# Placing transposed probabilities from two DMA queues in an attention and SoLU layer kernel

## The chip, the cores and the metric

The kernel runs on one core of one Trainium2 chip. The metric is the time of one execution on the device in microseconds (us), as the median of several runs. Beside the runs there is one execution recorded by the hardware profiler; its span, from the first to the last instruction, is what the views of the profile divide.

The core has five engines that each work through their own list of instructions in order: TensorE (PE, the matmuls), VectorE (DVE), ScalarE (ACT), GpSimd (POOL) and SyncE (SP, which only starts DMAs here). They meet through semaphores. ScalarE can start DMAs too.

## What is computed

Block-causal attention over 8 batches, 8 heads, 576 positions and 64 dimensions per head, and on its output, as 4608 tokens of 512, a layer with SoLU and a normalization:

```python
def _attn_ref(q, k, v):                       # (8, 8, 576, 64) each
    scores = scale * np.matmul(q, k.transpose(0, 1, 3, 2))
    mask = block_i >= block_j                 # blocks of 64 positions
    scores = np.where(mask, scores, -1000000000.0)
    scores = scores - np.max(scores, axis=-1, keepdims=True)
    attn = np.exp(scores)
    attn = attn / (np.sum(attn, axis=-1, keepdims=True) + 1e-09)
    return np.matmul(attn, v)

def _moe_ref(x, w_in, w_out, g_ln):           # x is (4608, 512), d_ff is 1024
    h = x @ w_in
    e = np.exp(h - np.max(h, axis=-1, keepdims=True))
    solu = h * e / (np.sum(e, axis=-1, keepdims=True) + 1e-09)
    ln = (solu - mean) / np.sqrt(var + 1e-06) * g_ln
    return ln @ w_out
```

The weights and g_ln come as float64 words and are taken apart on the chip.

## The kernel before, in words

**Two kinds of work.** Attention runs by pairs of heads, the layer by tiles of 128 tokens. A pair is two heads of one batch, so there are 32 pairs and 36 tiles. The four pairs of the first batch are worked in two parts (part 0 and part 1) so that the layer can begin early; the 28 pairs behind them are whole. This text numbers the pairs 0 to 31.

**A pair** (function `attention`): q and k are loaded and split into a high and a low part (`kh`, `kl`, `qh`, `ql`); PE forms the scores in groups of one query block of 128 rows per head (lines 567 and 573, written in this text as S128, S256, S384, S512 by their width, and L for the 64 last rows of both heads). DVE takes each row's maximum (L602), ACT the exponential with the row sum (L614), DVE adds and inverts the sums (L624, L625), and the probabilities `pb` are scaled by POOL, ACT or DVE (L632, L634, L633). For the AV product they are needed transposed. The first 8 entries (the parts of batch 0) are transposed by PE (L554). For the other 28 pairs DVE transposes 32x32 blocks in place (two instructions, L640: 12 and 13 slots of 128 columns), and four DMAs of 400 KB place the quarters of `pb` into the tile `pt` (L648, in `place`). PE then multiplies (L660, function `avmm`, 52 matmuls a pair in two results `av0` and `av1`), and ACT copies the results into the tile `xt` (L412, `copy`): one copy of 128x384 for `av0`, and three for `av1` (64x192, 64x128 and 64x64), because `av1`'s two halves stood at different columns. `pt`, `pb` and `vr` (the values v) have two buffers each, used in turn.

**A tile** (function `moe`): `xt` is split into `xh` and `xl` (L721, L725); two times 12 matmuls with w_in (L746, "H" here); maximum, exponential, product, mean (L752 to L761); the square sum on ACT (L764); DVE transposes 32x32 blocks (L782), four DMAs place them into `ct` (L786); `ct` is split into `ch` and `cl` (L794, L798); two times 12 matmuls with w_out (L816, "O" here); the result leaves through `ob` (L820, L822).

**What sets the order.** All operations are handed to `Schedule.op` with an engine (and others that could do it, `alts`), a duration, what they read and write, and a key. `Schedule.run` is a planner: it walks through a model of the five engines in time, and whenever an engine is free it gives it the ready operation with the smallest key. The keys are the number of the pair or tile plus a value of the table PARAMS. The order so found is the order in which the instructions are written, for every engine; nothing is chosen on the chip. For a DMA the planner holds a duration of the issue, a duration on the DMA engines (`dma`) and a latency (`tail`). Four placements were planned as 4 x 600 ns of issue, 6800 ns of transfer and 3200 ns of latency.

**Queues.** Before the change every DMA but the very first stands on SP's queue: loads of q, k (four DMAs each, 144 KB) and v, placements of `pt` (4 a pair) and of `ct` (4 a tile), and the results. What stands ahead in this queue must have been issued before the next one is.

The functions that the change touches, and what calls them:

Of the kernel before, what the change touches and what calls it, by code (L numbers as in the profile page):

```python
# [14 lines left out]
I32 = mybir.dt.int32  # L15
# [16 lines left out]
NPT = 2  # L32
# [5 lines left out]
DEPTH = 2500.0  # L38
SLACK = 120.0
START = {"PE": 0.0, "ACT": 2930.0, "DVE": 0.0, "POOL": 2500.0, "SP": 560.0}  # L40
PARAMS = {
# [6 lines left out]
    "a_sp": 15.151, "a_sp32": 33.434, "a_lf": -19.843, "a_w": -53.076, "a_xh": 7.699, "a_xl": 42.171,  # L48
    "a_c": 45.045, "a_o": 1.147, "np": 32, "l0": 10.919, "a_cl": 82.304, "a_ai": -19.611, "aff": -198.558,
    "a_t3": -226.025, "a_cm": -13.873, "a_cg": -136.828, "a_sa": -14.146, "a_sa32": 226.312, "a_qh": -1.948,  # L50
    "a_kl": -33.0, "a_ch": 8.609, "a_chd": 185.089, "a_clo": -87.939, "ct0": -0.422, "qA": -20.741,
    "qeA": -57.386, "sA": -4.436, "seA": -5.607, "srA": 89.822, "spA": 243.774, "ptA": 46.328, "peA": -58.037,
    "avA": 18.17, "aeA": 50.13, "ldA": -276.676, "lvA": 10.694, "a_spA": -0.83, "a_saA": 1.199, "w2": 5.397,
    "w3": 49.83, "hA": 84.857,
}
# [6 lines left out]
class Schedule:  # L62
# [49 lines left out]
    def run(self):  # L112
# [20 lines left out]
        while events:  # L133
# [18 lines left out]
            for e in engs:  # L152
# [46 lines left out]
                if best.dma > 0.0:  # L199
                    dmafree = max(t + min(best.dur, 600.0), dmafree) + best.dma  # L200
                    engfree[e] = max(done, dmafree - DEPTH)
                    done = max(engfree[e], dmafree)
                heapq.heappush(events, (done + best.tail, n, 1, best, None))
# [8 lines left out]
def kernel(  # L212
# [53 lines left out]
    wid[LAST] = S  # L266
    soff = {(0, 0): 0, (0, 1): 1, (0, 2): 3, (1, 0): 6, (1, 1): 7, (1, 2): 9, (0, 3): 12, LAST: 16, (1, 3): 21}
    NSL, NSA = 25, 12
# [57 lines left out]
    def t_act(n, extra=0.0):  # L326
        return n / 1.2 + 51.0 + extra
# [16 lines left out]
    def rows(dst, src):  # L344
        for r_ in range(4):
            SP.dma_start(dst[r_::4], src[r_])
# [7 lines left out]
    def prep(i, src, hi, lo, gcol, name, key):  # L354
# [7 lines left out]
        op("ACT", 520, lambda: ACT.activation(T3.bitcast(I32), raw[:, :, 0], AF.Copy, scale=2.0**-29), r=[kr_], w=[k3], key=key,  # L362
           alts=[("POOL", 640, lambda: POOL.tensor_scalar(out=T3.bitcast(I32), in0=raw[:, :, 0], scalar1=2.0**-29, scalar2=1.0, op0=ALU.mult, op1=ALU.mult), K["a_t3"])])
# [18 lines left out]

    op("SP", 4 * 500, lambda: rows(gt, g_ln.rearrange("(c r j) -> r j c", r=4, j=32)), w=["gt"], key=K["w2"], tail=2100)
    n = 0
# [25 lines left out]
    def copy(which, n_, aps, scale, w, key, ps, r=()):  # L410

        op("ACT", t_act(n_), lambda: ACT.activation(aps()[0], aps()[1], AF.Copy, scale=scale), r=r, w=w, key=key, ps=ps,  # L412
           alts=[("DVE", t_dve(n_), lambda: DVE.tensor_scalar(out=aps()[0], in0=aps()[1], scalar1=scale, scalar2=None, op0=ALU.mult), K[f"e{which}"])])
# [29 lines left out]
    def attention(p, pair, part=None):  # L443
# [86 lines left out]
        for x, z, hi, lo, scale in () if peq or part == 0 else (("k", kz[:, zs], kh_, kl_, 1.0), ("q", qz[:, zs], qh_, ql_, 0.125)):  # L530
            zk = (x + "z", zs)
            op("DVE", t_dve(S) + 30, lambda z=z: DVE.transpose(z, z), r=[zk], w=[zk], key=kk)
            op("ACT", t_act(S), lambda z=z, hi=hi, scale=scale: ACT.activation(hi, z, AF.Copy, scale=scale), r=[zk], w=[(x + "h", iq)], key=ke,
               alts=[("POOL", 0.836 * S + 243, lambda z=z, hi=hi, scale=scale: POOL.tensor_scalar(out=hi, in0=z, scalar1=scale, scalar2=1.0, op0=ALU.mult, op1=ALU.mult), K["a_qh"])])
# [24 lines left out]
        for g, (kind, us, masks) in enumerate(groups):  # L559
# [57 lines left out]
            if g in zlast:  # L617
# [9 lines left out]
                zk = [("z", i, u) for u in bs]  # L627
                op("DVE", 300, recip, r=zk, w=[("rz", i, zg)] + zk, key=p + K["sr" + sfx])
                for b in bs:
# [14 lines left out]
        if not pep:  # L644

            def place():
                for a_ in (0, 2, 1, 3):
                    SP.dma_start(pt_[:, a_].rearrange("p s i -> p (s i)"), pb[32 * a_ : 32 * a_ + 32].rearrange("p r s i -> p (r s i)"))  # L648

            op("SP", 4 * 600, place, r=tk, w=ptk, key=p + K["pe" + sfx], tail=3200, dma=6800)  # L650

# [5 lines left out]
        def avmm():  # L657
# [28 lines left out]
            for j in range(5):  # L686
                for h in range(2):
                    if j < 4:
                        sl = slice(12 + j, 17 + j, 4) if h == 0 else slice(16 + j, 22 + j, 5)
                        mm(av1, h, low(0), j, 2 * h, 2 * h + 2, sl, j == 0, False)  # L690
                    else:
                        mm(av1, h, flat(128 - 128 * h, 2), j, 2 * h, 2 * h + 2, 20, False, True)
            for j in range(4):
                for h in range(2):
                    mm(av1, h, flat(64, 2), j, 2 - 2 * h, 4 - 2 * h, 12 + 9 * h + j, j == 0, j == 3)

        d = 660 if part == 0 else 2500 if part else 2835
# [177 lines left out]
```

## Time and profile before

| | |
|---|---|
| runs, us | 731.9, 723.35, 724.76 |
| median, us | 724.76 |
| profiled execution, us | 728.37 |
| its span, us | 726.6 |
| mean granted TensorE clock | 0.974 |
| bytes read from and written to HBM | 37.23 MB, 9.44 MB |
| DMA packets on SP's queue, their share of 16 engines | 222320, 74.9% |
| matmuls, weight loads | 4747, 4747 |

The profiled execution took 728.37 us, 1.8 us more than its span; it is 0.5% above the median of the three runs and lies between them. Times in the views are counted in us from the span's start. A row that groups instructions gives the line, the engine, the operation and its tiles, the count, the busy time in us with the mean of one in ns, and behind the last bar the idle time of the engine just before them with what ended it. A row of the timeline gives start, duration, and in square brackets the idle time ahead of it.

### The profile page before, as it was taken

To read this page: it belongs to the slowest core of one execution; us is meant where nothing else is said; L and a number is where in the kernel's file an instruction comes from. 1 tells how busy PE (TensorE), PEld (TensorE's weight loads), DVE (VectorE), ACT (ScalarE), POOL (GpSimd) and SP (SyncE) were. 2 spreads that over 40 slices of the span, in tenths; PEclk is the share of its full clock that TensorE was granted. 3 is DMA by queue.
4 is the path that set the end of the run, shared out by engine and by line. 5 is a ranking of instruction groups with operands and counts; after the bars stand their busy time and mean duration, and the time that the engine had idled before them with its cause. 6 is when DMAs were issued, how large, how long until landed. Compare 5 with 4: busy or idle time off the path is not lost.

```text
span 726.6 us, 14364 instructions
## 1 busy us (share of the span) xinstructions
PE 673.5 (93%) x4747; PEld 530.2 (73%) x4747; DVE 574.3 (79%) x1252; ACT 499.8 (69%) x1286; POOL 359.6 (49%) x512
## 2 busy tenths in 40 slices
PE   5687897999999999989999999999989999999997
PEld 4565575777777777767777777777767777788885
DVE  2798989896999888978798979698878977455552
ACT  3686889686878867767786778587857885444432
POOL 1367566443665454546555554556456555223211
PEclk8598989999999999999999999999999999999999
DMA  9855358596969897969896989797969767322221
GB/s 172 195 96 130 99 114 141 123 130 169 165 170 174 213 176 194 155 166 172 203 172 163 176 205 158 173 187 180 179 160 188 171 167 168 105 72 72 73 73 44
DMA packets 223434, 109.74 MB, mean 151 GB/s; under 512 B 186496, under 2 KB 202368, under 8 KB 223360
## 3 DMA queue, kind: packets, MB, share of 16 engines
q1 hardware_dynamic: 222320, 108.56, 74.9%
q8 instruction: 37, 0.61, 0.4%
q10 hardware_dynamic: 1040, 0.26, 0.2%
q14 instruction: 37, 0.30, 0.1%
HBM read 37.23 MB, written 9.44 MB: 64 GB/s over the span
## 4 chain that ended last, share of the span: by engine, by line
PE 55%; DVE 12%; DMA 12%; ACT 9%; SPq 6%; issue 3%; POOL 2%; DVEq 0%; ACTq 0%; POOLq 0%
PE ps L816 20%; PE ps L746 16%; PE ps L660 9%; PE ps L573 6%; DMA pt<-pb 5%; ACT pb L614 3%; PE ps L567 3%; DVE nm L602 2%; DMA kz<-in_k_dram 2%; SPq L648 2%; DVE pb L640 2%; ACT pb L634 2%; DMA ct<-zb 2%; SPq L461 2%; DMA ub<-in_moe_w_in_dram 1%
## 5 line engine op out<-in xcount | busy, mean ns | idle before, releaser
L614 ACT ACTIVATE pb<-ps,nm 128x384 f32<-128x384 f32 (+4 forms) x288 | 157.1, 555 | 74.2 <-DVE nm L602 58.6
L602 DVE TENSOR_REDUCE nm<-ps 128x1 f32<-128x384 f32 (+4 forms) x288 | 132.1, 505 | 0.4
L640 DVE STREAM_TRANSPOSE pb<-pb 128x1536 f32<-128x1536 f32 (+1 forms) x56 | 101.6, 1829 | 11.4 <-ACT pb L634 7.8
L660 PE MATMUL ps<-pt,vr 128*64 128x128 f32 (+1 forms) x1648 | 92.6, 269 | 12.9 <-DMA ct<-zb 7.1
L660 PEld LDWEIGHTS ps<-pt,vr 128*64 128x64 f32 x1648 | 81.8, 137 | 30.8 <-issue 12.7
L634 ACT ACTIVATE pb<-pb,rz 128x512 f32<-128x512 f32 (+4 forms) x185 | 92.1, 566 | 17.4 <-DVE rz L625 14.5
L746 PE MATMUL ps<-wih,xh 128*128 128x512 f32 x288 | 84.3, 414 | 3.7 <-ACT pb L614 3.7
L798 POOL TENSOR_TENSOR cl<-ct,ch 128x512 fp32r<-128x512 f32 x40 | 51.6, 1293 | 71.0 <-ACT ch L794 69.0
L632 POOL TENSOR_SCALAR pb<-pb,rz 128x512 f32<-128x512 f32 (+4 forms) x101 | 63.9, 644 | 40.3 <-DVE rz L625 17.1
L816 PE MATMUL ps<-woh,ch 128*128 128x512 f32 x288 | 80.7, 402 | 0.0
L746 PE MATMUL ps<-wil,xh 128*128 128x512 f32 x288 | 79.5, 398 | 0.0
L816 PE MATMUL ps<-woh,cl 128*128 128x512 f32 x288 | 78.8, 395 | 0.0
L746 PE MATMUL ps<-wih,xl 128*128 128x512 f32 x288 | 78.7, 395 | 0.0
L816 PE MATMUL ps<-wol,ch 128*128 128x512 f32 x288 | 78.7, 395 | 0.0
L761 POOL TENSOR_SCALAR ub<-ub,ms 128x1024 f32<-128x1024 f32 x31 | 35.7, 1151 | 82.7 <-DVE ms L755 68.5
L573 PE MATMUL ps<-kh,qh 64*128 64x128 f32 (+3 forms) x256 | 58.3, 386 | 11.4 <-ACT pb L614 7.5
L746 PEld LDWEIGHTS ps<-wih,xh 128*128 128x128 f32 x288 | 50.9, 190 | 23.8 <-issue 8.6
L746 PEld LDWEIGHTS ps<-wil,xh 128*128 128x128 f32 x288 | 54.8, 190 | 13.0
L746 PEld LDWEIGHTS ps<-wih,xl 128*128 128x128 f32 x288 | 54.3, 189 | 13.1 <-POOL xl L725 0.3
L816 PEld LDWEIGHTS ps<-woh,cl 128*128 128x128 f32 x288 | 54.2, 188 | 12.8
L816 PEld LDWEIGHTS ps<-wol,ch 128*128 128x128 f32 x288 | 54.2, 188 | 12.8
L816 PEld LDWEIGHTS ps<-woh,ch 128*128 128x128 f32 x288 | 51.5, 188 | 11.4 <-ACT pb L614 0.4
(124 smaller groups left out, 1299.3 us busy)
## 6 DMA issues: line engine op xcount, KB each, us to landing
pt<-pb SPq DMA_DIRECT2D x112, 400.0 KB, 6.1
ct<-zb SPq DMA_DIRECT2D x124, 128.0 KB, 2.7
out_dram<-ob SPq DMA_DIRECT2D x36, 256.0 KB, 3.1
vr<-in_v_dram SPq DMA_DIRECT2D x64, 128.0 KB, 3.8
qz<-in_q_dram SPq DMA_DIRECT2D x56, 144.0 KB, 4.7
kz<-in_k_dram SPq DMA_DIRECT2D x56, 144.0 KB, 3.9
ub<-in_moe_w_in_dram SPq DMA_DIRECT2D x8, 512.0 KB, 6.6
ub<-in_moe_w_out_dram SPq DMA_DIRECT2D x16, 256.0 KB, 3.2
```

The source lines that it names most:

```text
L567: PE.matmul(t[:, 192 + k0 : 192 + k1], w_, x_[:, k0:k1], start=n_ == 0, stop=n_ == 2)
L573: PE.matmul(PS(sps[h])[:, off : off + 128 * (i_ + 1)], w_[half[h], 128 * i_ : 128 * i_ + 128], x_[half[h], 0 : 128 * (i_ + 1)], start=n_ = ...
L602: op("DVE", t_dve(wid[u]), lambda sp=sp, off=off, u=u: DVE.tensor_reduce(out=nm_[u], in_=PS(sp)[:, off : off + wid[u]], axis=AX.X, op=ALU. ...
L614: ACT.activation(dst, src, AF.Exp, bias=nm_[u], accum_out=z_[zg][:, zc : zc + 1])
L632: op("POOL", 0.836 * nn + 243, lambda b=b, zg=zg, zc=zc: POOL.tensor_scalar(out=puv(pb, b, pep), in0=puv(pb, b, pep), scalar1=rz_[zg][:, z ...
L634: ("ACT", t_act(nn, 133), lambda b=b, zg=zg, zc=zc: ACT.activation(puv(pb, b, pep), puv(pb, b, pep), AF.Copy, scale=rz_[zg][:, zc : zc + 1 ...
L640: op("DVE", 1.058 * 128 * (s1 - s0) + 86, lambda s0=s0, s1=s1: DVE.transpose(pb[:, :, s0:s1, :], pb[:, :, s0:s1, :]), r=[("P", i, b) for b ...
L660: PE.matmul(dst(PS(av)[half[h]]), w_, pt_[:, a0:a1, sl, :], start=start, stop=stop)
L746: PE.matmul(o_, a_[:, c, :], w_[:, c, s_], start=(si == 0 and c == 0), stop=(si == 2 and c == NKI - 1))
L761: op("POOL", 1097, lambda: POOL.tensor_scalar(out=dst, in0=src, scalar1=m[:, 3:4], scalar2=1.0, op0=ALU.add, op1=ALU.mult), r=[uk, ("m3", ...
L798: alts=[("POOL", 1225, lambda c_=c_, h_=h_, l_=l_: POOL.tensor_tensor(out=l_, in0=c_, in1=h_.bitcast(F32), op=ALU.subtract), K["a_clo"])])
L816: PE.matmul(o_, a_[:, c, :], w_[:, c, :], start=(hf == 0 and si == 0 and c == 0), stop=(hf == 1 and si == 2 and c == 7))
```

## The change

Three things are changed.

1. **Placement.** `place` becomes two operations: SP issues the DMAs of quarters 0 and 1, ACT those of quarters 2 and 3. Both read what the four read. The AV product waits for both.
2. **One copy for `av1`.** The slots of `pb` and the columns of `av1` are numbered anew, so that both halves of `av1` hold 192 columns in the same order, and one copy of 128x192 takes the place of three. The number of matmuls is the same.
3. **Planner.** Some durations are corrected, the DMA engines' time of a pair of placements is now 2400 ns, the latency 2600 ns, an issue on ACT does not hold ACT for the transfer; the whole table PARAMS has other values, so the order changes on every engine.

The core of the diff:

```diff
-    soff = {(0, 0): 0, (0, 1): 1, (0, 2): 3, (1, 0): 6, (1, 1): 7, (1, 2): 9, (0, 3): 12, LAST: 16, (1, 3): 21}
+    soff = {(0, 0): 0, (0, 1): 1, (0, 2): 3, (1, 0): 6, (1, 1): 7, (1, 2): 9, (0, 3): 12, (1, 3): 16, LAST: 20}
...
                     dmafree = max(t + min(best.dur, 600.0), dmafree) + best.dma
-                    engfree[e] = max(done, dmafree - DEPTH)
-                    done = max(engfree[e], dmafree)
+                    if e == "SP":
+                        engfree[e] = max(done, dmafree - DEPTH)
+                    done = max(done, dmafree)
...
-            def place():
-                for a_ in (0, 2, 1, 3):
-                    SP.dma_start(pt_[:, a_].rearrange("p s i -> p (s i)"), pb[32 * a_ : 32 * a_ + 32].rearrange("p r s i -> p (r s i)"))
-
-            op("SP", 4 * 600, place, r=tk, w=ptk, key=p + K["pe" + sfx], tail=3200, dma=6800)
+            def place(eng, a0):
+                for a_ in (a0, a0 + 1):
+                    eng.dma_start(pt_[:, a_].rearrange("p s i -> p (s i)"), pb[32 * a_ : 32 * a_ + 32].rearrange("p r s i -> p (r s i)"))
+
+            op("SP", 1200, lambda: place(SP, 0), r=tk, w=ptk, key=p + K["pe" + sfx], tail=2600, dma=2400)
+            op("ACT", 1050, lambda: place(ACT, 2), r=tk, w=[("ptB", p % NPT)], key=p + K["pf" + sfx], tail=2600, dma=2400)
...
-        for av, rows, parts in ((av0, both, [first]), (av1, half[0], [(0, 384, 192)]), (av1, half[1], [(64, 384, 128), (0, 512, 64)])):
-            for c_, q_, l_ in parts if av else ():
+        for av, rows, (c_, q_, l_) in ((av0, both, first), (av1, both, (0, 384, 192))):
+            if av:
```

The order of the instructions, at three places. Numbers behind a tile's name tell its buffers apart (`pb_88` and `pb_89`, `pt_90` and `pt_91`); line numbers of the changed kernel are 1 higher up to L649 and 4 higher from L725 on.

**SP's queue, two pairs in the steady middle.** `out_dram` is a tile's result, `ct<-zb` the placement in the layer. Before:

```order
L648 DMA pt_91<-pb_89 128x1x800 x4
L822 DMA out_dram<-ob_131 128x512
L786 DMA ct<-zb 128x1x256 x4
L461 DMA kz<-in_k_dram 32x36x32 x4
L461 DMA qz<-in_q_dram 32x36x32 x4
L472 DMA vr_81<-in_v_dram 128x4x64 x2
L476 DMA vr_81<-in_v_dram 64x2x64
L648 DMA pt_90<-pb_88 128x1x800 x4
```

The changed kernel, at the same place:

```order
L649 DMA pt_91<-pb_89 128x1x800 x2
L826 DMA out_dram<-ob_131 128x512
L790 DMA ct<-zb 128x1x256 x4
L462 DMA kz<-in_k_dram 32x36x32 x4
L462 DMA qz<-in_q_dram 32x36x32 x4
L473 DMA vr_81<-in_v_dram 128x4x64 x2
L477 DMA vr_81<-in_v_dram 64x2x64
L649 DMA pt_90<-pb_88 128x1x800 x2
```

The order on SP is the same; two placements of each pair have left it.

**ACT, the steady middle, around the copies of one AV product.** `ub` is the exponential of a layer tile, `nm_24` belongs to the group L, the other `nm` to the groups S. Before:

```order
L412 ACTIVATE xt_118<-ps_63 128x384
L412 ACTIVATE xt_118<-ps_64 64x192
L412 ACTIVATE xt_118<-ps_64 64x128
L412 ACTIVATE xt_118<-ps_64 64x64
L614 ACTIVATE pb_88,z_1_111<-ps_61,nm_24_100 128x5x4x32
L820 ACTIVATE ob_131<-ps_65,ms_133 128x512
```

The changed kernel, at the same place of a pair:

```order
L413 ACTIVATE xt_120<-ps_64 128x384
L413 ACTIVATE xt_120<-ps_65 128x192
L649 DMA pt_90<-pb_88 128x1x800 x2
L757 ACTIVATE ub,ms_132<-ps_61,ms_132 128x1024
L615 ACTIVATE pb_89,z_1_113<-ps_62,nm_24_109 128x5x4x32
L615 ACTIVATE pb_89,z_0_112<-ps_66,nm_02_103 128x3x4x32
```

ACT now issues two placements right behind the copies of the AV product of the pair before; the exponentials of the next pair and of a layer tile stand behind them.

**ACT, the start of the kernel.** `ob<-ub` takes apart the first weights as soon as they have arrived. Before:

```order
L614 ACTIVATE pb_88,z_0_110<-ps_63,nm_00_92 128x128
L362 ACTIVATE ob_131<-ub 128x512
L614 ACTIVATE pb_88,z_0_110<-ps_64,nm_11_97 128x256
L366 ACTIVATE zb<-zb 128x512
L412 ACTIVATE kh_84<-ps_66 128x256
L412 ACTIVATE qh_82<-ps_66 128x256
L614 ACTIVATE pb_88,z_0_110<-ps_64,nm_10_96 128x128
```

The changed kernel, from the same exponential on:

```order
L615 ACTIVATE pb_88,z_0_110<-ps_63,nm_00_92 128x128
L615 ACTIVATE pb_88,z_0_110<-ps_64,nm_11_97 128x256
L615 ACTIVATE pb_88,z_0_110<-ps_64,nm_10_96 128x128
L635 ACTIVATE pb_88<-pb_88,rz_0_114 128x256
L413 ACTIVATE kh_84<-ps_66 128x256
L413 ACTIVATE qh_82<-ps_66 128x256
L413 ACTIVATE pt_90<-ps_64 128x4x96
```

The work on the weights no longer stands between the exponentials of the first pair; on ACT it comes 13 instructions later. On SP the first load of w_in, which stood ahead of g_ln and the first loads of v, now stands behind them.

Who does what changes as well. Counted over the whole order: scalings of `pb` go from 101 on POOL, 185 on ACT and 2 on DVE to 27, 159 and 102; `ch<-ct` from 62 on ACT to 21 on ACT, 32 on POOL and 9 on DVE; the 36 copies `ob<-ps` of the layer's result from 27 on ACT and 9 on DVE to 36 on ACT.

More of the change, by code (lines that the diff above doesn't have):

```diff
@@ L41 @@
 PARAMS = {
[6 rows of a table removed]
[L48 to L54, printed above, removed]
[6 rows of a table added]
+    "e2": 6.854, "a_sp": -5.24, "a_sp32": -2.39, "a_lf": 392.26, "a_w": -42.859, "a_xh": -1.838,
+    "a_xl": -1.31, "a_c": 108.552, "a_o": 24.452, "np": 32, "l0": -2.145, "a_cl": 58.245, "a_ai": -18.732,
+    "aff": 163.937, "a_t3": -246.666, "a_cm": 104.43, "a_cg": -6.932, "a_sa": -81.936, "a_sa32": -235.294,
+    "a_qh": -173.369, "a_kl": 2.08, "a_ch": -31.735, "a_chd": -13.936, "a_clo": -282.32, "ct0": 158.564,
+    "qA": 77.049, "qeA": 0.58, "sA": -293.262, "seA": -14.134, "srA": -1.22, "spA": -15.414, "ptA": 6.678,
+    "peA": 111.138, "avA": 29.198, "aeA": 156.22, "ldA": -86.586, "lvA": -114.061, "a_spA": -9.618,
+    "a_saA": -115.183, "w2": -69.111, "w3": -46.994, "hA": 532.627, "pf": 8.694, "pf32": -9.701, "pfA": 16.29,
 }
@@ L361, in prep @@
         high = raw[:, :, 1].bitcast(F32)
-        op("ACT", 520, lambda: ACT.activation(T3.bitcast(I32), raw[:, :, 0], AF.Copy, scale=2.0**-29), r=[kr_], w=[k3], key=key,
+        op("ACT", 570, lambda: ACT.activation(T3.bitcast(I32), raw[:, :, 0], AF.Copy, scale=2.0**-29), r=[kr_], w=[k3], key=key,
            alts=[("POOL", 640, lambda: POOL.tensor_scalar(out=T3.bitcast(I32), in0=raw[:, :, 0], scalar1=2.0**-29, scalar2=1.0, op0=ALU.mult, op1=ALU.mult), K["a_t3"])])
@@ L381, in prep @@
         wkeys.append((name, "l"))
-    op("SP", 4 * 500, lambda: rows(gt, g_ln.rearrange("(c r j) -> r j c", r=4, j=32)), w=["gt"], key=K["w2"], tail=2100)
+    op("SP", 4 * 500, lambda: rows(gt, g_ln.rearrange("(c r j) -> r j c", r=4, j=32)), w=["gt"], key=K["w2"], tail=2100, dma=2800)
     n = 0
@@ L410, in copy @@
     def copy(which, n_, aps, scale, w, key, ps, r=()):
-        op("ACT", t_act(n_), lambda: ACT.activation(aps()[0], aps()[1], AF.Copy, scale=scale), r=r, w=w, key=key, ps=ps,
+        op("ACT", t_act(n_, 100 if n_ < 200 else 0), lambda: ACT.activation(aps()[0], aps()[1], AF.Copy, scale=scale), r=r, w=w, key=key, ps=ps,
            alts=[("DVE", t_dve(n_), lambda: DVE.tensor_scalar(out=aps()[0], in0=aps()[1], scalar1=scale, scalar2=None, op0=ALU.mult), K[f"e{which}"])])
@@ L532, in attention @@
             op("DVE", t_dve(S) + 30, lambda z=z: DVE.transpose(z, z), r=[zk], w=[zk], key=kk)
-            op("ACT", t_act(S), lambda z=z, hi=hi, scale=scale: ACT.activation(hi, z, AF.Copy, scale=scale), r=[zk], w=[(x + "h", iq)], key=ke,
+            op("ACT", t_act(S, 44), lambda z=z, hi=hi, scale=scale: ACT.activation(hi, z, AF.Copy, scale=scale), r=[zk], w=[(x + "h", iq)], key=ke,
                alts=[("POOL", 0.836 * S + 243, lambda z=z, hi=hi, scale=scale: POOL.tensor_scalar(out=hi, in0=z, scalar1=scale, scalar2=1.0, op0=ALU.mult, op1=ALU.mult), K["a_qh"])])
@@ L627, in attention @@
                 zk = [("z", i, u) for u in bs]
-                op("DVE", 300, recip, r=zk, w=[("rz", i, zg)] + zk, key=p + K["sr" + sfx])
+                op("DVE", 300, recip, r=zk, w=[("rz", i, zg)] + zk, key=p + K["sr" + sfx], port=True)
                 for b in bs:
@@ L666, in low, with flat2 @@
                 return lambda t: t[:, c0 : c0 + 256].rearrange("p (s a i) -> p a s i", s=2, a=4)[:, 0:2]
+            def flat2(c0):
+                return lambda t: t[:, c0 : c0 + 128].rearrange("p (s a i) -> p a s i", s=2, a=2)
             def flat(c0, n_):
@@ L688, in avmm @@
                     if j < 4:
-                        sl = slice(12 + j, 17 + j, 4) if h == 0 else slice(16 + j, 22 + j, 5)
-                        mm(av1, h, low(0), j, 2 * h, 2 * h + 2, sl, j == 0, False)
+                        mm(av1, h, low(0) if h == 0 else flat2(64), j, 2 * h, 2 * h + 2, slice(12 + 4 * h + j, 21 + j, 8 - 4 * h), j == 0, False)
                     else:
-                        mm(av1, h, flat(128 - 128 * h, 2), j, 2 * h, 2 * h + 2, 20, False, True)
+                        mm(av1, h, flat(128, 2), j, 2 * h, 2 * h + 2, 24, False, True)
             for j in range(4):
                 for h in range(2):
-                    mm(av1, h, flat(64, 2), j, 2 - 2 * h, 4 - 2 * h, 12 + 9 * h + j, j == 0, j == 3)
+                    mm(av1, h, flat(64 - 64 * h, 2), j, 2 - 2 * h, 4 - 2 * h, 12 + 4 * h + j, j == 0, j == 3)
         d = 660 if part == 0 else 2500 if part else 2835
-        op("PE", d, avmm, r=ptk + [("pt2", p % NPT, s_) for s_ in slots] + ([("v0", c) for c in range(2)] + [("qz", c) for c in range(2)] if part == 0 else [f"vr{i}"]), key=kk, opens=av0 if part == 0 else (av0, av1), mode=1)
+        op("PE", d, avmm, r=ptk + [("pt2", p % NPT, s_) for s_ in slots] + [("ptB", p % NPT)] + ([("v0", c) for c in range(2)] + [("qz", c) for c in range(2)] if part == 0 else [f"vr{i}"]), key=kk, opens=av0 if part == 0 else (av0, av1), mode=1)
         both = slice(0, P)
         first = {None: (0, 0, 384), 0: (0, 0, 256), 1: (256, 256, 128)}[part]
-        for av, rows, parts in ((av0, both, [first]), (av1, half[0], [(0, 384, 192)]), (av1, half[1], [(64, 384, 128), (0, 512, 64)])):
-            for c_, q_, l_ in parts if av else ():
+        for av, rows, (c_, q_, l_) in ((av0, both, first), (av1, both, (0, 384, 192))):
+            if av:
                 w_ = [("xt", b0 % XB, hp, rows.start, q0) for q0 in (0, 256, 384, 512) if q_ <= q0 < q_ + l_]
@@ L715, in moe @@
         m = ms[i]
-        pieces = [(0, 0, 256), (0, 256, 384), (0, 384, 576), (64, 384, 512), (64, 512, 576)]
+        pieces = [(0, 0, 256), (0, 256, 384), (0, 384, 576)]
         xk = [("xt", x, hp, r0, q0) for x, a0, a1, _, _ in segs for hp in range(NP) for r0, q0, q1 in pieces if q0 < a1 and q1 > a0]
```

12 rows, old and new, of the table PARAMS are left out of this document.

## The prediction

> **What bounds the kernel now.** I read the page's first part, then the windows by stage, then PE's waits in the longest stage.
>
> ```profile
> span 726.6 us, 14364 instructions
> PE 673.5 (93%) x4747; PEld 530.2 (73%) x4747; DVE 574.3 (79%) x1252; ACT 499.8 (69%) x1286; POOL 359.6 (49%) x512
> ```
>
> ```profile
> 0.00:40.00 40.00, 25.73 (x237) 21.96 (x239) 22.42 (x66) 20.00 (x63) 11.27 (x25) 0.70 0.81 167
> 40.00:140.00 100.00, 83.17 (x685) 64.43 (x686) 92.63 (x210) 80.53 (x205) 63.61 (x82) 0.93 0.58 121
> 140.00:200.00 60.00, 58.68 (x424) 45.72 (x423) 49.00 (x113) 45.65 (x125) 28.56 (x47) 1.00 0.87 152
> 200.00:600.00 400.00, 383.84 (x2801) 300.17 (x2800) 342.22 (x746) 300.56 (x798) 221.32 (x314) 1.00 0.92 177
> 600.00:727.00 127.00, 122.11 (x607) 97.93 (x606) 68.08 (x122) 53.05 (x100) 34.81 (x47) 1.00 0.32 87
> ```
>
> The columns are the stretch, its length, the busy time of PE, PEld, DVE, ACT and POOL, the granted clock, the DMA engines' share and GB/s. PE bounds the kernel: 93% of the span. Its idle time is 53.1 us (726.6 - 673.5), and the change leaves the matmuls as they are, so that is all there is to gain. It lies at the start (14.3 us up to 40 us, 16.8 up to 140), in the steady stage from 200 to 600 (16.2) and at the end (4.9). From 40 to 140 DVE is busier than PE (92.63 against 83.17).
>
> In the steady stage PE's own waits are these:
>
> ```profile
> PE ps L660 <- DMA ct<-zb: 7.1, 4, 2.6
> PE ps L660 <- DMA pt<-pb: 4.1, 4, 1.2
> PE ps L573 <- ACT pb L614: 3.5, 7, 1.5
> PE ps L567 <- DVE ub L754: 1.2, 1, 1.2
> ```
>
> 11.2 of the 16.2 us are the AV product's (L660), eight times, 2.6 us at most. AV does not read `ct`; the first row is the same wait put down to a DMA that landed a little later. One such wait, followed back through SP's queue:
>
> ```profile
> 404.30 3.57 DVE L640 STREAM_TRANSPOSE pb<-pb 128x1536 f32<-128x1536 f32 x2 [0.26 <-ACT pb L634]
> ...
> 425.28 2.92 PE L660 MATMUL ps<-pt,vr 128*64 128x128 f32 x50 [1.17 <-DMA pt<-pb]
> ```
>
> ```profile
> 398.79 1.79 SPq L822 DMA_DIRECT2D out_dram<-ob  x1
> 400.69 3.63 SPq L786 DMA_DIRECT2D ct<-zb  x4
> 404.41 2.78 SPq L461 DMA_DIRECT2D kz<-in_k_dram  x4
> 407.30 4.16 SPq L461 DMA_DIRECT2D qz<-in_q_dram  x4
> 411.56 1.62 SPq L472 DMA_DIRECT2D vr<-in_v_dram  x2
> 413.23 0.64 SPq L476 DMA_DIRECT2D vr<-in_v_dram  x1
> 413.97 5.70 SPq L648 DMA_DIRECT2D pt<-pb  x4
> ```
>
> DVE has both transposes done at 407.87, but SP starts the placement at 413.97, 6.1 us late: it was issuing what stands ahead, and just before this stretch stand the four placements of the pair before. AV then starts at 425.28, 1.17 us late. So AV waits for SP's queue. One placement by itself:
>
> ```profile
> 413.97 0.56 SPq L648 DMA_DIRECT2D pt<-pb  x1
> ```
> ```profile
> 414.57 0.63 SPq L648 DMA_DIRECT2D pt<-pb  x1
> ```
> ```profile
> 415.26 3.16 SPq L648 DMA_DIRECT2D pt<-pb  x1
> ```
> ```profile
> 418.46 1.20 SPq L648 DMA_DIRECT2D pt<-pb  x1
> ```
>
> The first two issues take 0.56 and 0.63 us, the third is held 3.16 and the fourth 1.20: behind two placements the queue takes no more until the first has moved.
>
> **The change part by part.**
>
> *SP.* The third and fourth issue leave SP: 3.16 + 1.20 = 4.36 us a pair. The order on SP is otherwise the same, so the placement after this stretch can begin 4.36 us sooner, at 409.6 and not 413.97, still behind the transposes (407.87). The longest AV wait is 2.6 us, so all eight go if the rest stays. I take 10 of the 11.2 us. Bounds: 0 if landing, not issue, sets the wait; 11.2 if all go.
>
> *ACT's issues.* 56 DMAs. The nearest rows are the first two issues above and ACT's only one:
>
> ```profile
> 0.72 0.47 ACTq L435 DMA_DIRECT2D xt<-in_k_dram  x1
> ```
>
> At 0.59 each (mean of 0.56 and 0.63) they are 33 us of ACT; 26 at the low row. If ACT met the held issues, a pair would cost 4.36 and not 1.19 us (the first rows' sum), 89 us more over 28 pairs; I take the low price, since the third issue is held behind two on its own queue, and ACT's queue gets only two a pair. The issue waits for DVE's transposes. Behind it on ACT stand the exponential of a layer tile and those of the next pair's L and S384, for whose PSUM PE waits. Their maxima stand behind the transposes on DVE as well, so this wait adds little: 0, with the issue time of 1.2 us a pair hidden under the AV-to-scores work of PE.
>
> *ACT's other work.*
>
> ```profile
> L412 ACT ACTIVATE xt<-ps 64x192 f32<-64x192 f32 x32 | 10.2, 318 | 2.5 <-PE ps L660 2.4
> L412 ACT ACTIVATE xt<-ps 64x128 f32<-64x128 f32 x32 | 8.7, 272 | 0.4
> L412 ACT ACTIVATE xt<-ps 64x64 f32<-64x64 f32 x32 | 6.6, 208 | 0.0
> L794 ACT ACTIVATE ch<-ct 128x512 fp32r<-128x512 f32 x62 | 38.8, 629 | 8.5 <-DMA ct<-zb 6.0 <-PE ps L816 2.2 <-issue 0.3
> ```
>
> Three copies (25.5 us in all) become one of the first row's width: 32 x 0.318 = 10.2, so 15 us are saved. 41 `ch` leave ACT: 41 x 0.629 = 26 us. The issues add 33. ACT ends within some 15 us of now and was busy 300.56 of 400 us in the steady stage: nothing on the path, as PE's work covers it; with no cover, the copy of `av1` alone would free its PSUM bank 0.48 us sooner a pair.
>
> *DVE.* 100 more scalings of `pb`. The rows that price them:
>
> ```profile
> L633 DVE TENSOR_SCALAR pb<-pb,rz 128x256 f32<-128x256 f32 x1 | 0.3, 346 | 0.0
> L633 DVE TENSOR_SCALAR pb<-pb,rz 128x128 f32<-128x128 f32 x1 | 0.3, 286 | 0.0
> L369 DVE TENSOR_SCALAR ct<-ct 128x512 uint32<-128x512 uint32 x8 | 3.4, 423 | 0.0
> L821 DVE TENSOR_SCALAR ob<-ps,ms 128x512 f32<-128x512 f32 x9 | 6.5, 721 | 0.0
> ```
>
> At 0.36 (the widths lie between the first and third row) 36 us, less 9 x 0.721 = 6.5 for the `ob` copies that leave, plus 9 `ch` at 0.42: about 33 us, some 28 of it in the steady stage: 342.22 becomes 370 of 400, 93%. In sum it fits under PE's 384; what it may cost is a maximum that comes late. I take 2 us, bounds 0 and 28 (1 us in each pair). POOL loses 74 scalings and stays under its 221 of 400: 0.
>
> *The start.*
>
> ```profile
> 22.85 0.47 PE L554 MATMUL ps<-ident,pb 128*128 128x128 f32 x1 [9.29 <-ACT pb L634]
> ```
> ```profile
> 16.22 0.68 ACT L362 ACTIVATE ob<-ub 128x512 int32<-128x512 uint32 x1 [3.62 <-DMA ub<-in_moe_w_in_dram]
> ```
> ```profile
> 5.73 1.53 SPq L350 DMA_DIRECT2D ub<-in_moe_w_in_dram  x2
> 7.30 2.77 SPq L346 DMA_DIRECT2D gt<-in_moe_g_ln_dram  x4
> ```
>
> PE's longest wait, 9.29 us, ends with a scaling that stood behind ACT's work on the weights; ACT itself sat 3.62 us for their DMA, between two exponentials of the first pair. In the new order that work comes after the first scalings, so the first transposes can start earlier. Against it, the weights are loaded behind g_ln (2.77 us of issue) and v, and up to 140 us DVE has little to spare. Bounds: 9.3 gained (the whole wait) and 2.8 lost (all that follows the weights later by g_ln's issue). I take 4 gained, a little under the middle between the whole gain and none.
>
> *The AV matmuls* keep number and size: 0. The other waits of the steady stage, 4.7 us, I leave as they are.
>
> *Sum* against the profiled execution: 728.4 - 10 + 2 - 4 = 716.4. That execution was 3.6 us above the median of the runs (724.76), so the forecast for the median is **713 us**: 12 us less. A change of 2%, 14.5 us, is about what a measurement of this kernel can tell from none; that is below 710.3 or above 739.3.
>
> **The rivals.**
>
> *The start gains more.* The first 9.29 us wait goes wholly, and with it lost clock:
>
> ```profile
> 14.00:37.50 23.50, 13.12 (x94) 10.95 (x96) 16.78 (x47) 13.62 (x45) 7.49 (x8) 0.50 0.81 168
> ```
>
> The clock is halved from the wait on: 13.12 us of PE work at 0.50 could have been 6.6. For it: the wait's cause is moved away. Against it: DVE. Start 14 in place of 4: 703 us. (The Trainium skill, "TensorE: Matmul & The Clock Gate", Part 1, says that an idle window of about 3.4 us halves the clock; this trace agrees with the half clock behind a 9.29 us wait. By that rule a wait of some 2 us would leave the clock whole.)
>
> *The transfers are no faster, the wait stays.* Over one placement and the loads around it the DMA engines are full:
>
> ```profile
> 414.00:425.20 11.20, 10.12 (x47) 7.39 (x47) 10.46 (x22) 9.55 (x25) 7.28 (x9) 1.00 0.95 206
> ```
>
> At a share of 0.95 two queues move nothing sooner, and what SP issues next is held instead. Half or more of AV's wait stays and only the start gains: 713 + 9 = 722 us. Against it: the late start on SP, which is not a transfer. The Trainium skill, "DMA: Bandwidth & Descriptors", section "Issuing engines are not separate DMA queues", states this rule: DMAs from several engines run on the same 16 engines, and several issuers save only the issue time. The trace's 0.95 agrees. By that rule only the 4.36 us of issue are saved, which in my sum is already all that counts.
>
> *Slower: DVE's transposes as one block.* In the new order both transposes of a pair stand together (3.57 us as above) behind the five scalings that ACT and DVE share, and ahead of the maxima of the next tile and pair. If that block ends late, the exponentials, the PSUM banks and then PE's next scores and H matmuls are late in each of 28 pairs. It decides from 0.43 us a pair (then the 12 us are gone) and makes the kernel slower by over 2% from 0.95. At 1 us a pair: 713 + 28 = 741 us. For it: DVE at 93%. Against it: now there is only one wait of 1.2 us of that kind (L567).
>
> *Slower still: ACT meets the held issue.* 89 us more on ACT, of which its 99 idle us in the steady stage cover about half: 713 + 44 = 757 us. Against it: the first two issues of each pair on SP are short though other DMAs run.
>
> **How the numbers follow.** Forecast 713, from 706 to 720: 0.42. Start gains more, 703: 0.20. Wait stays, 722: 0.18. DVE's block, 741: 0.12. Held issue, 757: 0.05. Something else near no change: 0.03. Faster by over 2%: 0.20 and 0.4 of the forecast's 0.42 (the part of its 14 us band below 710.3, rounded up), 0.37. Slower: 0.05 and three quarters of 0.12, 0.14. Same: the rest, 0.49. The range goes from 699 (the start's rival less 4) to 732 (the wait's rival and ten more, which takes in some of DVE's block): it leaves out 0.05, most of 0.12 and a few hundredths below.
>
> **What would show it.** Right: AV's waits for DMAs in the steady stage under 3 us in all; SP's two issues about 0.6 each and ACT's two as well; `pt` issued within 3 us of the transposes' end in every pair; PE's wait before the first L554 (now L555) under 4 us. Wrong: ACT issues of 1.2 to 3 us; PE's waits for ACT's exponentials or DVE's maxima over 15 us in the steady stage; DVE busy less than 350 of 400 us there with the time still longer; a start as long as now, with DVE waiting for w_in.

## The result, and the profile after

| | before | changed |
|---|---|---|
| median of the runs (us) | 725.56 | 798.02 |
| lowest and highest (us) | 723.35 to 731.9 | 791.06 to 801.71 |
| profiled execution: time, span (us) | 728.4, 726.6 | 801.71, 799.6 |
| PE busy, idle (us) | 673.5, 53.1 | 696.4, 103.2 |
| mean granted clock | 0.974 | 0.942 |

The changed kernel takes 1.0971 times as long (95% interval 1.088 to 1.1062): 9.7% slower, where 1.7% faster was forecast and the range ended at 732. The head of the changed kernel's page, and its windows (columns as in the prediction):

```profile
span 799.6 us, 14182 instructions
PE 696.4 (87%) x4747; PEld 547.1 (68%) x4747; DVE 579.3 (72%) x1343; ACT 467.6 (58%) x1178; POOL 326.9 (41%) x465
```
```profile
0.00:40.00 40.00, 29.34 (x287) 23.78 (x287) 23.17 (x75) 25.99 (x78) 10.31 (x25) 0.83 0.77 166
40.00:140.00 100.00, 83.06 (x651) 65.73 (x652) 89.88 (x207) 80.87 (x195) 46.65 (x64) 0.90 0.53 111
140.00:200.00 60.00, 53.35 (x387) 41.27 (x386) 46.37 (x110) 39.64 (x110) 16.79 (x26) 0.94 0.81 149
200.00:600.00 400.00, 351.07 (x2441) 273.81 (x2440) 309.78 (x719) 237.70 (x614) 190.52 (x267) 0.96 0.83 158
600.00:800.00 200.00, 179.60 (x987) 142.50 (x985) 110.11 (x235) 83.37 (x182) 62.61 (x85) 0.96 0.45 99
```

PE has as many matmuls as before (x4747), but 50 us more idle time, most of it in the steady stage: 48.9 of 400 us idle (400 - 351.07), before 16.2. Another 15 us came up behind 600 us: 20.0 us idle (199.6 - 179.60), before 4.9. The rest of the 73 us of span is a lower clock: 673.5 x 0.974 and 696.4 x 0.942 are both 656.0, so the 23 us more of busy time are the same work at a lower clock.

PE's waits in the steady stage (us in total, times, longest):

```profile
PE ps L662 <- DMA pt<-pb: 19.7, 9, 4.9
PE ps L820 <- ACT pb L615: 15.3, 7, 3.2
PE ps L750 <- ACT pb L615: 6.6, 3, 2.9
PE ps L574 <- ACT pb L615: 4.3, 1, 4.3
```

AV's waits for the placement (L662), which were to go, grew from 11.2 to 19.7 us, and the waits for ScalarE's exponentials (L615) grew from 3.5 to 26 us. Two rows on SyncE's queue and one on ScalarE tell where both begin:

```profile
SPq L473 <- DMA pt<-pb: 48.5, 10, 5.6
SPq L477 <- DMA pt<-pb: 12.4, 9, 1.8
```
```profile
ACT ob L768 <- DMA out_dram<-ob: 91.2, 28, 7.7
```

The first two rows did not exist before: SyncE's loads of v (L473, L477) wait for placements. They do not read `pt`. In the traces every DMA of this program reports its landing on one of eight semaphores, which go round over the DMAs of both queues, and waits until the one that had its semaphore last has landed. ScalarE's two placements now take two of the eight. The third row was 26.8 us before (14 times): the square (L768) writes to the scratch `ob`, whose result a store is still reading. One placement shows the first of the two; here are the transposes on DVE, ScalarE's issues, and SyncE's queue:

```profile
401.29 3.56 DVE L641 STREAM_TRANSPOSE pb<-pb 128x1536 f32<-128x1536 f32 x2
```
```profile
404.88 1.21 ACTq L649 DMA_DIRECT2D pt<-pb  x2
```
```profile
404.31 5.93 SPq L473 DMA_DIRECT2D vr<-in_v_dram  x2
411.97 0.65 SPq L477 DMA_DIRECT2D vr<-in_v_dram  x1
412.71 1.20 SPq L649 DMA_DIRECT2D pt<-pb  x2
414.01 2.68 SPq L826 DMA_DIRECT2D out_dram<-ob  x1
416.78 4.21 SPq L790 DMA_DIRECT2D ct<-zb  x4
```

ScalarE issues its half as soon as the transposes end (404.85). SyncE's second load of v has the semaphore of ScalarE's first placement, its third load that of the second, so both stand until these have landed, and SyncE's own half goes out at 412.71, 7.8 us after the other: the halves go one after the other. In 15 of the 28 pairs SyncE's half begins 4 us or more behind ScalarE's. In all, SyncE stood 72.8 us in 23 such waits. Where no such load stands ahead, both queues issue together, and ScalarE is held:

```profile
426.92 3.00 ACTq L649 DMA_DIRECT2D pt<-pb  x2
```

The first issue took 0.59, the second 2.38 us. Over 28 pairs the issues took ScalarE 49.4 us, in 10 pairs for more than 2 us.

### The profile page after: what moved, and what is told of

It reads as the page before. It is cut to its first block, busy times and chain, and to the rows that moved or that the text cites. A ratio compares the mean times of both kernels' runs of the same rounds, so it can differ in the third digit from the quotient of the medians.

```text
span 799.6 us, 14182 instructions
## 1 busy us (share of the span) xinstructions
PE 696.4 (87%) x4747; PEld 547.1 (68%) x4747; DVE 579.3 (72%) x1343; ACT 467.6 (58%) x1178; POOL 326.9 (41%) x465
## 4 chain that ended last, share of the span: by engine, by line
PE 30%; DMA 28%; DVE 14%; ACT 12%; SPq 7%; issue 5%; ACTq 2%; POOL 2%; DVEq 0%; POOLq 0%
PE ps L820 12%; DMA pt<-pb 10%; DMA out_dram<-ob 10%; PE ps L662 7%; PE ps L750 6%; ACT pb L615 5%; DMA qz<-in_q_dram 3%; DVE nm L603 3%; DVE pb L641 3%; PE ps L574 3%; SPq L462 2%; ACTq L649 2%; ACT pb L635 2%; ACT ob L768 2%; DVE kz L533 1%
## 5 line engine op out<-in xcount | busy, mean ns | idle before, releaser
L615 ACT ACTIVATE pb<-ps,nm 128x256 f32<-128x256 f32 (+4 forms) x288 | 157.1, 558 | 50.1 <-DVE nm L603 39.0
L603 DVE TENSOR_REDUCE nm<-ps 128x1 f32<-128x512 f32 (+4 forms) x288 | 132.5, 505 | 0.7
L662 PE MATMUL ps<-pt,vr 128*64 128x128 f32 (+1 forms) x1648 | 101.8, 284 | 34.0 <-DMA pt<-pb 23.4
L662 PEld LDWEIGHTS ps<-pt,vr 128*64 128x64 f32 x1648 | 89.3, 147 | 55.1 <-issue 27.5
L820 PE MATMUL ps<-woh,ch 128*128 128x512 f32 x288 | 85.8, 421 | 27.4 <-ACT pb L615 25.4
L635 ACT ACTIVATE pb<-pb,rz 128x128 f32<-128x128 f32 (+4 forms) x159 | 83.0, 594 | 5.2 <-DVE rz L626 5.0
L768 ACT ACTIVATE ob<-ub 128x1024 bf16<-128x1024 f32 x31 | 32.8, 1057 | 87.6 <-DMA out_dram<-ob 87.6
L820 PE MATMUL ps<-wol,ch 128*128 128x512 f32 x288 | 83.5, 414 | 0.0
L757 ACT ACTIVATE ub<-ps,ms 128x1024 f32<-128x1024 f32 x36 | 40.2, 1117 | 50.4 <-DVE ps L599 18.4
L802 POOL TENSOR_TENSOR cl<-ct,ch 128x512 fp32r<-128x512 f32 x45 | 57.9, 1288 | 26.8 <-ACT ch L798 14.7
```

The source lines that it names most:

```text
L603: op("DVE", t_dve(wid[u]), lambda sp=sp, off=off, u=u: DVE.tensor_reduce(out=nm_[u], in_=PS(sp)[:, off : off + wid[u]], axis=AX.X, op=ALU. ...
L615: ACT.activation(dst, src, AF.Exp, bias=nm_[u], accum_out=z_[zg][:, zc : zc + 1])
L635: ("ACT", t_act(nn, 133), lambda b=b, zg=zg, zc=zc: ACT.activation(puv(pb, b, pep), puv(pb, b, pep), AF.Copy, scale=rz_[zg][:, zc : zc + 1 ...
L662: PE.matmul(dst(PS(av)[half[h]]), w_, pt_[:, a0:a1, sl, :], start=start, stop=stop)
L757: op("ACT", t_act(1024, 186), lambda: ACT.activation(u, PS(hps), AF.Exp, bias=m[:, 0:1], accum_out=m[:, 1:2]), r=[("m0", i)], w=[uk, ("m1" ...
L768: op("ACT", t_act(1024, 135), lambda: ACT.activation(ob[i].bitcast(mybir.dt.bfloat16), cz, AF.Square, accum_out=m[:, 4:5]), r=[ck], w=[("m ...
```

## The experiments

Theory S: the scratch `ob` costs. Theory Q: the queues cost, by the semaphores that they share. Theory O: the new order is worse on every engine. Theory A came later: what stops ScalarE costs. In the names of the kernels a stands for the changed kernel and b for the kernel before. Each kernel was measured against the kernel before, on its chip.

**Scratch and queue by themselves, in both orders.**

```diff
 a_sq, b_sq (the changed kernel, the kernel before)
-ACT.activation(ob[i].bitcast(bf16), cz, AF.Square, ...)
+ACT.activation(sqo.bitcast(bf16), cz, AF.Square, ...)
 a_sp (the changed kernel)
-op("ACT", 1050, lambda: place(ACT, 2), ...)
+op("ACT", 1050, lambda: place(SP, 2), ...)
 b_split (the kernel before)
-SP.dma_start(pt_[:, a_]...)
+(SP if a_ < 2 else ACT).dma_start(pt_[:, a_]...)
```

a_sq: 

> The changed kernel, with the square of the gated rows written to a tile of its own instead of to the scratch `ob`, whose last result a store is still reading; order and queues stay. Theory S (scratch: ScalarE's 91.2 us of waits for the store from `ob` are what costs) expects 725 to 745. Theory Q (queues: SyncE's loads wait for the completion of ScalarE's placements, 72.8 us in 23 waits, and the halves of a placement go one after the other) expects 785 to 800, since the same time is then lost at AV. Theory O (the new priorities give a worse order on every engine) expects 780 to 800.

a_sp: 

> The changed kernel with all four placements issued by SyncE, the second two at the place in the program where ScalarE issued them; priorities, order and layout stay. Theory Q expects 725 to 750: no load waits for a placement of ScalarE, and SyncE's held third issue comes back. Theory S expects 790 or more, because a store then stands behind four placements instead of two. Theory O expects 785 to 800.

b_split: 

> The kernel before with its own priorities and order, and only this changed: of the four placements two are issued by ScalarE, at the same place of the program. Theory Q expects 750 to 800, slower by itself. Theory S expects 720 to 735, since in this order the square comes some 19 instructions after the scaled result, far from its store. Theory O expects 710 to 728, the gain of 10 us that was forecast, at least in part.

b_sq: 

> The kernel before, with the square written to a tile of its own. Its ScalarE waited 26.8 us in 14 waits for the store from `ob`. Theory S expects 705 to 718, theories Q and O 720 to 728: these waits lie beside matmuls that are ready.

Measured: a_sq 762.09 us (1.0485, 1.0419 to 1.055), a_sp 791.71 (1.0894, 1.0826 to 1.0962), b_split 768.74 (1.0591, 1.0503 to 1.068), b_sq 723.74 (0.9951, 0.9906 to 0.9995). So the scratch costs 36 us in the new order and about 3 in the old one (0.4 to 6.8 by the interval). S is right about half of the loss, though all three ranges for a_sq were missed. The order says why. From 300 to 650 us of the changed kernel the squares of `ob_131`, every second one, stand two instructions of ScalarE behind the result that they overwrite, and those of the other buffer 6 to 12. Before, in the steady stage, the distance was 10 or more where ScalarE wrote the result, and DVE wrote the rest. In the changed kernel:

```
L824 ACTIVATE ob_131<-ps_65,ms_133 128x512
L534 ACTIVATE kh_84<-kz 128x576
L768 ACTIVATE ob_131,ms_133<-ub 128x1024
```

a_sp is a miss for Q: all four on SyncE brings back 6 us only. But b_split is one for O, and for S: in the old order the split alone makes the kernel 43 us slower.

**Both undone, and what else is in the order.**

```diff
 a_sp_sq: a_sp and a_sq together
 b_pf, b_split_pf: on SyncE, with the order otherwise as it was
-loads of q and v, pt
+pt, loads of q and v
 b_av1: of the change only
-for av, rows, parts in (..., (av1, half[0], [...]), (av1, half[1], [...])):
+for av, rows, (c_, q_, l_) in ((av0, both, first), (av1, both, (0, 384, 192))):
```

a_sp_sq: 

> The changed kernel with both: all four placements issued by SyncE, and the square written to a tile of its own, so that only the new priorities, durations and the one copy of AV's second result are left. By sums, 792 less the 36 us that the tile of its own was worth with two queues gives 756. If the order is at fault only by putting the square behind the store (theory S), 722 to 735. If the order is worse in other ways too (theory O), 745 to 765. If SyncE's queue was what cost (Q), under 740.

b_split_pf: 

> The kernel before with two placements on ScalarE's queue (768.7 us so), and one thing more: SyncE issues its own two placements ahead of the loads of queries and values that stood before them, not after. Then no placement of SyncE stands behind a load that waits for the completion semaphore of ScalarE's placements. Theory Q (the loads' waits for those semaphores put the halves one after the other) expects 725 to 742. If it is the issues on ScalarE themselves, or its queue of work, that cost, 760 to 772, since these stay.

b_pf: 

> Control for the last one: the kernel before with all four placements on SyncE, put ahead of the same loads. No load there waits for a placement of another engine, so theory Q expects 720 to 732, no change. If putting placements first is worth much by itself, 705 to 718, and if the later loads cost, 735 or more.

b_av1: 

> The kernel before with only AV's second result in one copy instead of three (slots, tiles' row halves and their matmuls as in the change), its priorities and durations kept; the order is made anew by the same rules. ScalarE and VectorE save some 30 us of copies that lie beside matmuls. If a new order by itself does not cost, 718 to 730; if any order that is not fitted to it loses time (theory O in its general form), 740 to 790.

Measured: a_sp_sq 766.87 (1.059, 1.0517 to 1.0663), b_split_pf 861.82 (1.1871, 1.1809 to 1.1934), b_pf 832.03 (1.1463, 1.1408 to 1.1518), b_av1 753.49 (1.0385, 1.0336 to 1.0434). a_sp_sq lies 2 us above O's range, and b_av1 in that of O's general form. b_pf spoils the pair as a test of Q: the control itself lost 106 us. Its SyncE queue shows it:

```profile
SPq L648 <- DVE pb L640: 100.7, 17, 21.4
```

The placement waits for the transposes (28.9 us before), and now the loads wait behind it. The pair still says one thing: beside its control the split costs 30 us here, though SyncE waited for ScalarE's placements only 7.6 us; so semaphores on SyncE cannot be all of a split's cost. ScalarE's second issue was held in 25 of 28 pairs here, and the issues took it 78.6 us in all. b_av1 removes two copies a pair, and the order that the same rules then give is 28 us slower.

**The same order with other semaphores.** For each of ScalarE's placements the order in which semaphores are handed out is tied to SyncE's last DMA ahead of it in the program; the instructions and their order are the same on every engine. (In b_lane the four placements are also written in the order 0, 1, 2, 3 and not 0, 2, 1, 3, which leaves the order on each engine as it was.)

```diff
+if x.engine == E_.Activation and o_.dma and "SP" in last:   # b_lane: o_.eng == "SP"
+    tc.add_manual_dep(x, last["SP"], NS)                    # order of issue only, no wait
```

b_lane: 

> The kernel before with two of four placements on ScalarE (768.7 us as tried), and the same instructions in the same order on every engine; only the completion semaphores, of which eight go round over the DMAs of both queues, are handed out in another order: ScalarE's placements get theirs behind SyncE's of the same pair, so that no load ahead of SyncE's placements waits for them. Theory Q (these waits put the halves one after the other in every second pair) expects 715 to 735. If ScalarE's issues, or placements late in its queue of work, are what cost, 760 to 772, no change.

b_lane_sq: 

> The same, and the square written to a tile of its own (worth 3 us in the kernel before). Theory Q with S expects 708 to 728, the fastest of all so far if the split is worth the 10 us that were forecast; without Q 755 to 770.

a_lane: 

> The changed kernel with the same instructions in the same order on every engine, and the completion semaphores of ScalarE's placements handed out right behind the loads of values before them instead of among the loads of queries. Theory Q expects 765 to 785 (13 to 33 us of 798 come back: a pair of halves that lies 9 us apart costs about 4 us of matmuls in 7 to 8 of the pairs of pairs); theory O with S alone 792 to 800.

a_lane_sq: 

> The same with the square in a tile of its own (762 us with the semaphores as they were). Theory Q expects 735 to 752; theory O alone 757 to 766, since one queue for all four gave 767 in this order too.

Measured: b_lane 758.04 (1.0459, 1.0398 to 1.0519), b_lane_sq 761.5 (1.0476, 1.0444 to 1.0507), a_lane 772.38 (1.0646, 1.058 to 1.0713), a_lane_sq 745.07 (1.0257, 1.0214 to 1.03). In the traces of a_lane and b_lane no wait of SyncE for a placement of ScalarE is left (72.8 us in the changed kernel, 75 in b_split). In the changed kernel Q's part is 26 us (17 once the scratch is out of the way), as expected. In the old order only 11 of 43 come back, so Q alone does not explain the loss there; but the 11 are a net figure, since waits for semaphores came up on ScalarE instead (below). What is left shows in b_lane's trace. SyncE from the placement to the last load of v, first before, then in b_lane:

```profile
353.06 5.67 SPq L648 DMA_DIRECT2D pt<-pb  x4
358.83 2.90 SPq L472 DMA_DIRECT2D vr<-in_v_dram  x2
361.78 0.68 SPq L476 DMA_DIRECT2D vr<-in_v_dram  x1
```
```profile
365.68 1.19 SPq L648 DMA_DIRECT2D pt<-pb  x2
366.98 6.31 SPq L472 DMA_DIRECT2D vr<-in_v_dram  x2
373.34 1.61 SPq L476 DMA_DIRECT2D vr<-in_v_dram  x1
```

9.40 us before (353.06 to 362.46) and 9.27 with the split (365.68 to 374.95): SyncE is freed of two issues, and its next DMAs are held for as long instead. So it is in all nine pairs in which these loads stand directly behind the placement: 9.37 to 10.06 us before, 9.10 to 9.67 in b_lane. ScalarE at the same place:

```profile
365.69 2.98 ACTq L648 DMA_DIRECT2D pt<-pb  x2
368.71 0.98 ACT L412 ACTIVATE xt<-ps 128x384 f32<-128x384 f32 x3 [2.46 <-DVE nm L602]
```

The copies start when the second issue is out, whatever releaser the row names. The hold goes with the other queue: ScalarE's second issue took 2.29 to 3.20 us in the 15 pairs in which SyncE's first began at most 0.05 us behind ScalarE's first, and 0.55 to 0.87 in the 13 in which it began 0.24 us or more behind. In b_lane ScalarE is stopped 91.6 us in this way: 61.0 in issues, of which 15 are held over 2 us, and the rest in waits ahead of them and between them, 24.7 us of these for semaphores that SyncE's loads of q had last: handed out the other way round, they make ScalarE wait for SyncE. That is theory A.

**Theory A by itself.**

```diff
 b_stall (the kernel before, four placements on SyncE; b_stall1: once, not three times)
+ACT.activation(sqo, pb[:, 0:1024], AF.Copy)   # x3
 b_lane31: b_lane with
-(SP if a_ < 2 else ACT).dma_start(...)
+(SP if a_ < 3 else ACT).dma_start(...)
```

b_stall: 

> The kernel before, all four placements on SyncE, and in ScalarE's program, where b_split and b_lane had its two placements, three copies of 128x1024 of the probabilities to a scratch instead: they wait for the same transposes and hold ScalarE for some 2.7 us, with no transfer. (It does work that nobody reads.) In b_lane ScalarE's placements stopped it for 91.6 us in 28 pairs, 3.3 each. If that stop is what a split costs in this order (theory A: exponentials behind it come late, and matmuls with them), 745 to 760. If the cost comes from the transfers or from SyncE's queue, 725 to 735.

b_lane31: 

> As b_lane, but ScalarE issues one of the four placements and SyncE three: same order on every engine, semaphores behind SyncE's of the same pair. One issue takes ScalarE 0.6 us, and the second, which was held for 2.3 to 2.5 us in 15 of 28 pairs, is gone. Theory A expects 730 to 745, between 726 and 758, by the stop that is left (about a third). If any wait of ScalarE for the transposes is enough, 750 to 760.

b_stall1: 

> As b_stall, with one copy of 1.06 us in each pair instead of three: with its wait for the transposes some 1.3 us, 35 us in all, about what two issues of 0.55 and 0.62 us cost ScalarE when nothing holds them. (The copy is work that nobody reads.) If the cost goes with the length of the stop (32 us for 95 us of it), 735 to 741. If ScalarE has slack for so much, as the forecast took it, 724 to 730. If any stop at this place of the program costs the whole, 750 or more.

Measured: b_stall 758.26 (1.044, 1.0385 to 1.0496), b_lane31 762.09 (1.0515, 1.0446 to 1.0585), b_stall1 729.56 (1.0026, 0.9995 to 1.0058). With no transfer on ScalarE's queue and no semaphore shared with it, a stop of 3.4 us a pair gives b_lane's time, as theory A expects. PE's waits in the steady stage, in b_stall and in b_lane:

```profile
PE ps L573 <- ACT pb L614: 8.7, 17, 1.0
PE ps L746 <- ACT pb L614: 5.5, 4, 1.4
```
```profile
PE ps L573 <- ACT pb L614: 16.0, 14, 3.7
PE ps L746 <- ACT pb L614: 4.3, 3, 2.6
```

Both wait for exponentials (L614) ahead of the scores (L573) and the layer's product (L746), 14 and 20 us, 3.5 us before. A stop of 1.3 us a pair costs nothing that can be told from none (b_stall1; PE's waits for exponentials ahead of the scores are 4.1 us there). So the cost does not go with the length: in this order ScalarE has slack for the bare issues and not for 3.4 us. A pair with a held issue stops it 2.9 us, close to that; what the held issues cost without the waits for semaphores was not run in this order. b_lane31 is a miss, above all that was expected: one issue of 0.6 us should have been nearly free. No issue is held there, but ten pairs wait 40 us in all ahead of the issue for the semaphore that a load of q had last, 2.2 to 5.7 us each time. So such waits alone can cost as much, though SyncE's queue, now with three placements, is not the same either.

**The order.**

```diff
 a_par_lane_sq: a_lane_sq with the priorities of the kernel before
-    "nd": 2, "ld": 117.485, "lv": -77.627, ...
+    "nd": 2, "ld": -4.623, "lv": -205.654, ...
```

> All that the change does to the code, with semaphores handed out behind the loads and the square in a tile of its own (745.1 us with the new priorities), but with the priorities of the kernel before (and those of the second half's placement set to its first's), so that the order is made by the old numbers from the new durations and layout. If the new priorities as such are at fault for the 19 us that a_lane_sq is still above before, 718 to 735. If an order only fits the program for which its numbers were searched, 750 to 790.

Measured: 799.63 (1.1011, 1.0948 to 1.1075), above both ranges. The new priorities are not bad: the old ones make the same program 55 us slower. In the new order the split even helps once its semaphores are out of the way: a_lane_sq takes 745 us and a_sp_sq, on one queue, 767. What the last 19 us between a_lane_sq and the kernel before consist of was not separated; its largest wait in the steady stage is this:

```profile
PE ps L750 <- ACT pb L615: 13.6, 8, 2.6
```

Of all these kernels only b_sq came out faster than the kernel before, by half a per cent (0.05 to 0.94).

## Why the prediction was wrong

*ScalarE's order, put at nothing: the step that failed.* The prediction judges ScalarE by its busy time, "nothing on the path, as PE's work covers it", and says of PE's waits: "The other waits of the steady stage, 4.7 us, I leave as they are." Of these, 3.5 us were waits for ScalarE's exponentials; they became 26. ScalarE's busy time did fall (499.8 to 467.6 us); what came late was the work behind its waits. The square behind its store alone is 25 to 36 us in this order (a_sq 36), the largest part of the loss that is shown. It could be read ahead: ScalarE already waited 26.8 us there, and the new order puts the square two instructions behind the result.

*ScalarE's issues.* "I take the low price, since the third issue is held behind two on its own queue, and ACT's queue gets only two a pair." The hold is not of one queue: with two placements on each, ScalarE's second issue took 2.38 us beside SyncE's 0.55 and 0.60. Nor does it end when the first placement lands: before, the held third issue was out at 418.42 us and the first placement landed at 419.60. What ends it was not found. The low price itself would have been free in the old order: 1.3 us a pair (b_stall1). The rival "ACT meets the held issue" gave 757 us with a chance of 0.05, and b_lane measures 758. That is luck: the rival put 4.36 us of issues on ScalarE in each pair, and b_lane has 2.2 (61.0 over 28) and waits for semaphores, which the rival did not have. In the changed kernel the issues took 49.4 us where 33 were counted; what these 16 us cost there was not separated.

*SyncE freed of 4.36 us.* Wrong in the same way: 9.27 us against 9.40. The forecast let the hold vanish; it went to the next DMAs on SyncE and to ScalarE. The Trainium skill, "DMA: Bandwidth & Descriptors", section "Issuing engines are not separate DMA queues", says that several issuers save only the issue time; in these rows SyncE did not save even that.

*"The order on SP is otherwise the same."* Nearly true: in every fourth pair of the steady stage the loads of v now stand ahead of the placement and not behind it. But the semaphores were not looked at: they cost 17 to 26 us of the 72, and they were in the trace of before too, as the number on which each DMA waits.

*DVE.* The scalings cost 40 us where 36 were counted, but other work left DVE, and its busy time grew by 5 us (574.3 to 579.3) and not by 33. In the steady stage it was busy 309.78 of 400 us, and none of PE's five largest waits there is for it. The rival of DVE's block has nothing for it.

*The start.* Right: the first transposes begin at 14.24 and not at 22.85 us, and the wait of 9.29 us ahead of them is gone:

```profile
14.24 0.62 PE L555 MATMUL ps<-ident,pb 128*128 128x128 f32 x3 [0.50 <-DVE pb L634]
```

A new wait for an exponential, 4.54 us, comes up at 25.02. At 40 us PE had 3.6 us more of work done (29.34, 25.73), where 4 were forecast. It was given back in 140 to 200 us, 53.35 against 58.68.

*Clock.* The sum counted waits and not what they do to the clock. Of the 73 us of span, 23 are PE's work at a lower clock: 0.46 us for each of the 50 us of idle time.

Of the 72 us of loss 53 are thus shown: 36 for the scratch and then 17 for the semaphores on SyncE, or 26 and 27 when the semaphores go first. The other 19 stay open between the new order and ScalarE's stops; these were not told apart there.

## What to carry to other kernels

A DMA that moves to a compute engine's queue costs that engine not only its bare issue but whatever holds the issue: the other queue's transfers, and the semaphores that both share. Ask how long a stop the engine can bear at that place, and try it with dummy work: in the old order 1.3 us a pair were free, 3.4 us cost 32. Where an order is made anew, read for each tile that is reused as a scratch how far its next writer stands from the DMA that still reads it; and judge an edit within a fixed order, since here even less work (b_av1) lost 28 us by the order alone.

## What the runs showed of the hardware

Short waits can lower the clock. In b_stall no wait of PE from 400 to 440 us is longer than 0.82 us, yet behind that one and one of 0.41 us, which ends at 421.34, the granted clock (the third column from the end) is halved for 3.41 us, from 421.60 to 425.01. In the 3.41 us ahead of that PE was busy 2.18 us:

```profile
420.00:422.00 2.00, 1.16 (x5) 0.76 (x6) 2.00 (x5) 1.54 (x8) 0.80 (x1) 0.90 0.89 270
422.00:424.00 2.00, 2.00 (x6) 1.16 (x5) 1.22 (x5) 1.49 (x6) 1.47 (x2) 0.50 0.74 222
424.00:426.00 2.00, 2.00 (x8) 1.53 (x8) 1.77 (x6) 2.00 (x7) 1.84 (x5) 0.75 0.56 135
426.00:428.00 2.00, 2.00 (x10) 1.63 (x9) 1.16 (x2) 1.90 (x4) 1.90 (x4) 1.00 1.02 197
```

The Trainium skill, "TensorE: Matmul & The Clock Gate", Part 1, asks for an idle window of about 3.4 us, and the prediction worked out by it that a wait of some 2 us leaves the clock whole; the measurement differs. It is one place, and the matmuls between and behind the two waits are 64 deep (64*128) where others are 128; whether the waits or these matmuls count is not told apart.

Busy time times clock lies between 650 and 663 us in all 18 kernels (654.1 for b_split_pf with 714.1 us at 0.916, 653.8 for b_sq with 674.7 at 0.969), so a wait is paid twice: once idle, and once more in matmuls at a lower clock. By a straight line through the 18 kernels each us of idle time goes with 0.36 us more of busy time; it is 0.46 in the changed kernel and 1.0 in b_lane, so it depends on where the waits lie.
